# Softmax weights of two more pairs turned on TensorE, conversions taken off GpSimd, norm read from PSUM

## The chip, the cores and the metric

One core of one Trainium2 chip. The metric is the device time of one execution in microseconds (us).

## The reference, cut to what matters

```python
scores = scale * q @ k^T; scores = where(mask, -1e9, scores)      # 2 batches, 12 heads, 448 x 448, causal
attn = exp(scores - max) / (sum + 1e-9); x = attn @ v              # x: 896 tokens x 768
xn = x / sqrt(mean(x * x) + 1e-6) * rms_g
x = (silu(xn @ w_gate) * (xn @ w_val)) @ w_out                     # 768 -> 1536 -> 768
return ((x @ w1) * (x @ w2)) @ w3 @ w_out2                         # 768 -> 1024 -> 1024 -> 768
```

All data are fp32.

## The kernel before, in words

Every fp32 matrix outside the scores is split into a high part (fp16, "hi") and the rest (bf16, "lo"), and every product is three 16-bit matmuls: hi*hi, hi*lo, lo*hi. The kernel has two parts.

*Part one, 0 to about 168 us.* Attention runs over 12 pairs of heads (`pair`: 6 for each batch). For a pair, TensorE (PE) makes four blocks of scores in fp32, VectorE (DVE) adds the mask and takes the minimum (L556), ScalarE (ACT) takes the exponential (L560). The softmax weights then have to be turned (transposed) before they meet V. There are two ways. `turn` (L591): four 128x128 fp32 transposes on PE into a bank (L596), then ACT takes hi (L599) and DVE takes lo from the bank (L601); four such turns make one pair. `send` (L605): hi (L442/443/444) and lo (L447/448) are taken first in SBUF, and a DMA on SyncE's queue (SP) turns both 16-bit halves (L608); three such transfers make one pair, two of 128 x 1536 and one of 128 x 1024 elements. `DA` and `DB` name the pairs that are sent. Then PE multiplies with V (720 small matmuls, "PV"), and DVE divides by the row sum (L657 to L661).

In the same part the product of the last two weight matrices is formed (`w_prime`: 384 matmuls of 384 columns, evicted by ACT at L516) and the first gate weights are read. Each weight piece comes by DMA into one of four `st` buffers (L459), and two DVE instructions and one ACT instruction rebuild an fp32 number from its 64-bit form (`fetch`, L461, L464, L468).

At the end of each batch `norm` scales by the root mean square: ACT sums squares (L669), DVE and GpSimd (POOL) make the reciprocal root, DVE spreads it into `diag` (L684), PE multiplies each 128 columns with it (six groups into three banks), ACT evicts the bank with the gain (L700), and hi and lo are taken from the evicted fp32. For the second batch `mix` (L711) forms the seven operand sums of a Strassen-Winograd product out of both batches.

*Part two, from 168.67 us to the end.* 1944 matmuls of 448 columns: 12 units of gate and value, the down projection, 8 units of w1 and w2, 3 units of the last product. Each unit's weights are fetched, summed (L482) and split; its seven products are joined by DVE (L818).

The order of all instructions comes from a planner (`Plan`): it walks the graph with a price for each operation on each engine that may do it, places every operation on an engine and in a row, and repeats this eight times with priorities from the walk before. `alt` lists the engines that may also do an operation; for hi parts these are DVE and POOL, for lo parts and sums POOL. Buffers of SBUF that DVE and POOL share are priced as a lock (`port`). PE gets idle fillers (L432) in the first 60 us where the walk sees a gap. The numbers at the head (`TP`, `PO`, `BIAS`, `THETA` and so on) set the first priorities and the willingness to move work.

Of the kernel before, what the change touches and what calls it, by code (L numbers as in the profile page):

```python
# [15 lines left out]
ALU = mybir.AluOpType  # L16
# [23 lines left out]

TP = 28.0521
WP0 = -244.6493
WPS = 48.9793
GVS = 6.4864
OS = 3.1806
AS = 4.3573
FS = -5.7914
PO = dict(dq=86.1608, dv=18.1427, vh=-4.1615, vl=31.153, sc=-23.1187, s3=-45.5392, hA=-61.1976, hl=15.902,
    hB=-24.2123, pv=19.2543, sq=-20.7221, nm=29.1952, wm=26.8125, ww=-36.4818, wx=25.6973, g=24.6307,
    a=-40.6597, o=14.4327, f=-41.7402, gm=-30.163, e=10.5623, ae=-45.2952, y=-25.9701, t1=23.8236,  # L50
    mx=19.799, dw=-6.0874)


PASSES = 8
BIAS = {"dve": 17.4016, "pool": 80.0945, "act": 139.3857}
THETA = 0.4843

DA, DB = range(3,12), range(3,12)

# [6 lines left out]
class Plan:  # L66
# [39 lines left out]
    def schedule(self, ways, deps, prio, forward):  # L106
# [71 lines left out]
        while done < n:  # L178
            t, e = min((max(free[e], first[e]), e) for e in free if ready[e] and e not in idle)
            i = next((i for _, i in ready[e] if avail[i][e] <= t and not declines(t, e, i)), None)  # L180
            if i is None:
                idle.add(e)
                continue
            if e == "dve" and ways[i][e][2] and port > t:
                i = next((q for _, q in ready[e] if avail[q][e] <= t and not ways[q][e][2]), i)
            idle.clear()
            done += 1
            pop(i)
            us, _, locks = ways[i][e]
            if e == "pe":  # L190
                while forward and t - free[e] > 0.5 and t < FILL and cols.get(int(free[e] / TICK), 0.0) < 1.15 * WARM:
                    warm.append(free[e])
                    free[e] += pe(free[e], 0.215, 1.0)
                t = max(t, free[e])
                us = pe(t, us, self.ops[i][3])
            if locks:
                t = max(t, port)
                port = t + us
            if e == "dve":
                locked = locks  # L200
            free[e] = t + us
            start[i], pick[i] = t, e
            for u in users[i]:
# [66 lines left out]
def dma_us(b):  # L270
    return b / 310.0e3


@with_exitstack
def fused_kernel(ctx: ExitStack, tc, qk, v, g, wgv, wo, wab, w3t, wout, out):
# [253 lines left out]
    def pair(b, gi):  # L529
# [144 lines left out]
    def norm(b):  # L674
# [11 lines left out]
            rstd[b].to_broadcast([P, NT, P]), op=ALU.mult), r=[("rstd", b), "ident"], w=["diag"], prio=pr, port=True)  # L686
        ys = {}
        for gi in (0, 3, 1, 4, 2, 5):
# [3 lines left out]
            def f(x4=x4, ps=ps):  # L692
# [261 lines left out]
```

## Time and profile before

| | us |
|---|---|
| time before, median of 3 | 550.02 (549.77 to 550.32) |
| the profiled execution's own time | 548.47 |
| its span, first to last instruction | 546.7 |
| busy: PE, DVE, ACT, POOL | 524.3, 495.8, 338.8, 237.5 |
| TensorE's granted clock, mean | 1.000 |

The profiled execution is 1.77 us longer than its span and 1.55 us shorter than the median of the runs. Busy PE includes matmuls in flight, so 96% busy is not 96% of PE's peak. The granted clock is at full speed, 2.4 GHz, in every slice but the very end.

### The profile page before, as it was taken

The numbers are of one execution on the slowest core, as the hardware profiler recorded it, in microseconds if no ns is written. First come the engines' busy times: TensorE is split into PE (matmuls) and PEld (weight loads), VectorE is DVE, ScalarE is ACT, GpSimd is POOL, SyncE is SP. The second block draws the span as 40 slices with busy tenths as digits, with TensorE's granted clock in tenths as the row PEclk, the third lists the DMA queues.
The fourth block names the chain that finished last, engine by engine and source line by source line (L and its number), as shares of the span: only waits on it lengthen the run. The fifth ranks groups of instructions, "written<-read, shape, count | busy, mean of one in ns | idle before, by whom it ended". The sixth has DMA issues, their size and how long they took to land.

```text
span 546.7 us, 9215 instructions
## 1 busy us (share of the span) xinstructions
PE 524.3 (96%) x3442; PEld 286.6 (52%) x3442; DVE 495.8 (91%) x909; ACT 338.8 (62%) x492; POOL 237.5 (43%) x198
## 2 busy tenths in 40 slices
PE   6899999999899999999999999999999999999997
PEld 4565565564666554444555455555555555454553
DVE  6999999989959999999999999899658999999953
ACT  5988887896678676557464767676336553633210
POOL 4534364676453837053656420140211846673400
PEclk9999999999999999999999999999999999999999
DMA  8888799999951133334242446517104211000021
GB/s 276 288 278 263 222 252 218 258 248 184 279 112 59 34 127 130 122 109 173 70 162 78 158 172 252 208 59 236 52 0 168 65 59 59 0 1 0 35 101 68
DMA packets 55197, 77.02 MB, mean 141 GB/s; under 512 B 39792, under 2 KB 41328, under 8 KB 55152
## 3 DMA queue, kind: packets, MB, share of 16 engines
q1 hardware_dynamic: 55152, 76.43, 48.1%
q8 instruction: 27, 0.44, 0.3%
q14 instruction: 18, 0.15, 0.1%
HBM read 64.23 MB, written 2.75 MB: 123 GB/s over the span
## 4 chain that ended last, share of the span: by engine, by line
PE 54%; DVE 23%; DMA 8%; issue 5%; ACT 3%; POOL 0%; DVEq 0%; SPq 0%; ACTq 0%
PE bank L486 54%; DVE arena L818 6%; DVE arena L447 6%; DMA arena<-arena 5%; DVE cv L468 3%; DVE st L482 3%; DVE cv L461 2%; DVE arena L482 2%; DMA st<-in_wout 2%; ACT st L464 1%; DMA st<-in_w3t 1%; DVE arena L556 1%; ACT arena L442 1%; ACT arena L560 1%; DVE arena L547 0%
## 5 line engine op out<-in xcount | busy, mean ns | idle before, releaser
L486 PE MATMUL bank<-arena 128*128 128x448 f16 (+10 forms) x2976 | 446.1, 315 | 14.7 <-ACT wpr L516 3.9
L486 PEld LDWEIGHTS <-arena 128*128 128x128 f16 x3048 | 248.8, 98 | 229.0 <-issue 22.1
L464 ACT ACTIVATE st<-st 128x768 uint16<-128x768 uint16 (+2 forms) x72 | 117.6, 1658 | 32.6 <-DVE cv L461 29.9
L818 DVE TENSOR_TENSOR arena<-bank,arena 128x448 f32<-128x448 f32 x161 | 92.1, 612 | 18.1 <-PE bank L486 17.8
L442 ACT ACTIVATE arena<-arena 128x448 f16<-128x448 f32 (+2 forms) x90 | 53.9, 612 | 40.4 <-DVE arena L482 27.8
L468 DVE SCALAR_TENSOR_TENSOR cv<-st,cv 128x768 int32<-128x768 int32 (+2 forms) x84 | 75.1, 903 | 2.8 <-ACT st L464 2.6
L448 POOL TENSOR_TENSOR arena<-arena 128x448 bf16<-128x448 f32 (+2 forms) x29 | 49.6, 1713 | 56.7 <-ACT arena L442 44.5
L486 PE MATMUL bank<-xs,arena 128*128 128x448 f16 x360 | 72.4, 353 | 1.7 <-ACT arena L815 1.1
L447 DVE TENSOR_TENSOR arena<-arena 128x448 bf16<-128x448 f32 (+2 forms) x80 | 61.2, 780 | 2.4 <-ACT arena L442 1.1
L442 ACT ACTIVATE arena<-cv 128x768 f16<-128x768 f32 (+2 forms) x61 | 41.0, 679 | 32.5 <-DVE cv L468 18.6
L461 DVE TENSOR_SCALAR cv<-st 128x768 int32<-128x768 int32 (+2 forms) x84 | 50.0, 600 | 7.3 <-DMA st<-in_wout 4.2
L448 POOL TENSOR_TENSOR arena<-cv,arena 128x384 bf16<-128x384 f32 (+2 forms) x31 | 44.4, 1434 | 24.8 <-ACT arena L442 24.2
L483 POOL TENSOR_TENSOR arena<-arena 128x448 f32<-128x448 f32 x23 | 30.1, 1314 | 35.6 <-DVE arena L818 21.3
L560 ACT ACTIVATE arena<-arena 128x384 f32<-128x384 f32 (+3 forms) x84 | 41.2, 518 | 5.8 <-DVE arena L556 5.2
L444 POOL TENSOR_SCALAR arena<-cv 128x384 f16<-128x384 f32 (+2 forms) x22 | 20.2, 918 | 55.7 <-DVE cv L468 31.1
L447 DVE TENSOR_TENSOR arena<-cv,arena 128x768 bf16<-128x768 f32 (+2 forms) x53 | 43.3, 824 | 0.8 <-POOL arena L444 0.7
L447 DVE TENSOR_TENSOR arena<-st,arena 128x1536 bf16<-128x1536 f32 (+1 forms) x25 | 42.1, 1682 | 0.1
L482 DVE TENSOR_TENSOR arena<-arena 128x448 f32<-128x448 f32 x57 | 37.5, 668 | 4.1 <-ACT arena L864 4.1
L442 ACT ACTIVATE arena<-st 128x1536 f16<-128x1536 f32 (+1 forms) x22 | 30.5, 1389 | 17.4 <-DVE st L482 7.7
L556 DVE CUSTOM_DVE_ANT_0 arena<-bank,arena 128x384 f32<-128x384 f32 (+3 forms) x84 | 35.7, 441 | 1.9 <-PE bank L486 1.2
L486 PEld LDWEIGHTS bank<-arena 64*128 64x128 f32 (+2 forms) x288 | 27.5, 178 | 19.0 <-issue 5.2
L815 ACT ACTIVATE arena<-bank 128x448 f32<-128x448 f32 x23 | 12.6, 546 | 25.3 <-PE bank L486 15.2
(69 smaller groups left out, 310.2 us busy)
## 6 DMA issues: line engine op xcount, KB each, us to landing
st<-in_wgv SPq DMA_DIRECT2D x24, 768.0 KB, 4.5
st<-in_wab SPq DMA_DIRECT2D x16, 768.0 KB, 4.4
st<-in_wo SPq DMA_DIRECT2D x12, 768.0 KB, 4.4
st<-in_w3t SPq DMA_DIRECT2D x16, 512.0 KB, 4.8
st<-in_wout SPq DMA_DIRECT2D x16, 384.0 KB, 3.9
arena<-in_qk SPq DMA_DIRECT2D x12, 448.0 KB, 5.1
arena<-in_v SPq DMA_DIRECT2D x12, 256.0 KB, 3.8
out_t<-arena SPq DMA_DIRECT2D x12, 224.0 KB, 1.9
```

The lines of the kernel that those rows point to most:

```text
L442: add("act", act_us(n), lambda: nc.scalar.activation(hi, src, AF.Copy), r=r, w=w, prio=prio, alt=(("dve", dve2_us(n), lambda: nc.vector.te ...
L447: add("dve", dve_us(n), lambda: nc.vector.tensor_tensor(lo, src, hi, op=ALU.subtract), r=r, w=w, prio=prio, port=True, alt=(("pool", pool_ ...
L448: port=True, alt=(("pool", pool_us(n), lambda: nc.gpsimd.tensor_tensor(lo, src, hi, op=ALU.subtract)),))
L461: add("dve", dve2_us(n), lambda: nc.vector.tensor_scalar(cv, hi, 3, 0x3FFFFFFF, op0=ALU.logical_shift_left, op1=ALU.bitwise_and), r=[ks], ...
L464: add("act", ACT_TOP * n - 0.08, lambda: nc.scalar.activation(b[:, :, 2], b[:, :, 1], AF.Copy, scale=1.0 / 8192, bias=-8191.0 / 16384), w= ...
L468: add("dve", dve_us(n), lambda: nc.vector.scalar_tensor_tensor(cv, hi, -0x3FFFFFF9, cv, op0=ALU.bitwise_and, op1=ALU.bitwise_or), r=[ks], ...
L482: add("dve", dve_us(n), lambda: nc.vector.tensor_tensor(out, a, b, op=op), port=True, alt=(("pool", pool_us(n) + 0.1, lambda: nc.gpsimd.te ...
L483: ("pool", pool_us(n) + 0.1, lambda: nc.gpsimd.tensor_tensor(out, a, b, op=op)),), **kw)
L486: nc.tensor.matmul(*a, **k)
L556: add("dve", dve_us(w), lambda: nc.vector.tensor_tensor_reduce(out=sc[:, :w], in0=ss[:, :w], in1=m, scale=-CSC, scalar=3.0e38, op0=ALU.add ...
L560: add("act", act_us(w) + 0.1, lambda: nc.scalar.activation(dst, sc[:, :w], AF.Exp, bias=mx[:, c:c + 1], scale=-1.0), r=[ksc, kmx + (c,)], ...
L818: add("dve", dve_us(S), lambda: nc.vector.tensor_tensor(dst, ps, y, op=ALU.add), r=[kp, ky], w=[kd], prio=p)
```

## The change

- `DA`, `DB`: pairs 5 to 11 are sent by DMA instead of 3 to 11. Pairs 3 and 4 are turned on PE: 6 transfers fewer (27 to 21), 32 transposes of 128x128 more (48 to 80).
- POOL is no longer among the engines of `hi_part` and of V's conversion.
- `norm` no longer evicts the bank to fp32 and splits that: ACT takes hi straight from the bank (`halves`), DVE takes lo, and the differences of `mix`, straight from the bank (`less`, a scalar_tensor_tensor of 448 columns).
- The planner's prices: a transfer that turns 768 columns costs 1.9 us in place of 1.8, one of 512 columns 1.8 in place of 1.4; a plain transfer bytes/390e3 + 0.1 us in place of bytes/310e3, landing 2.4 us later in place of 2.0; POOL waits for the lock before it is given work, and a locked instruction costs 0.02 us more; fillers go where PE would idle over 0.3 us in the first 50 us.
- All numbers at the head are fitted anew, so the order on every engine changes.

```diff
-DA, DB = range(3,12), range(3,12)
+DA, DB = range(5,12), range(5,12)
...
-            t, e = min((max(free[e], first[e]), e) for e in free if ready[e] and e not in idle)
+            t, e = min((max(free[e], first[e], port if e == "pool" else 0.0), e)
+                       for e in free if ready[e] and e not in idle)
...
             if locks:
+                us += TURN
                 t = max(t, port)
...
-LAT = {"pe": 0.25, "sp": 2.0, "dve": 0.12, "act": 0.12, "pool": 0.12}
+LAT = {"pe": 0.25, "sp": 2.4, "dve": 0.12, "act": 0.12, "pool": 0.12}
...
-    return b / 310.0e3
+    return b / 390.0e3 + 0.1
...
     def hi_part(n, hi, src, r, w, prio):
         add("act", act_us(n), lambda: nc.scalar.activation(hi, src, AF.Copy), r=r, w=w, prio=prio, alt=(
-            ("dve", dve2_us(n), lambda: nc.vector.tensor_copy(hi, src)),
-            ("pool", n * 0.00115 + 0.05, lambda: nc.gpsimd.tensor_scalar(hi, src, 1.0, 1.0, op0=ALU.mult, op1=ALU.mult))))
+            ("dve", dve2_us(n), lambda: nc.vector.tensor_copy(hi, src)),))
...
-                 [ktA + (c, j) for c in range(3)], 1.8, t0 + PO["hA"])
+                 [ktA + (c, j) for c in range(3)], 1.9, t0 + PO["hA"])
...
+            def less(dst, kd, y, ky, ps=ps, kp=kp, gc=gc):
+                add("dve", dve_us(S), lambda: nc.vector.scalar_tensor_tensor(
+                    dst, ps[:, :S], gc, y, op0=ALU.mult, op1=ALU.subtract), r=[kp, ky, "gcol"], w=[kd], prio=pr)
+
+            def halves(s, i, ps=ps, kp=kp, gc=gc, less=less):
+                (hi, kh), (lo, kl) = xs(s, i, 0), xs(s, i, 1)
+                add("act", actp_us(S), lambda: nc.scalar.activation(hi, ps[:, :S], AF.Copy, scale=gc),
+                    r=[kp, "gcol"], w=[kh], prio=pr)
+                less(lo, kl, hi, kh)
...
-            if b == 0:
-                part(y, ky, xs, gi // 3, gi % 3, pr)
-            elif gi >= 3:
-                mix(xs, gi % 3, (y0[gi % 3], ("y0", gi % 3)), ys[gi % 3], (y0[gi], ("y0", gi)), ys[gi], pr)
+            if b:
+                t1s[gi] = ew_r.next()
+                less(*t1s[gi], y0[gi], ("y0", gi))
+            else:
+                halves(gi // 3, gi % 3)
```

What the new numbers do to the order is seen at three places. The first is SP's queue where the sent pairs begin: `in_wout` are the last weights of `w_prime`, `in_wgv` the first of the gate units, `in_qk` and `in_v` a pair's inputs. Before:

```order
L459 DMA st3_74<-in_wout 128x768
L540 DMA arena_69<-in_v 128x512
L459 DMA st1_72<-in_wout 128x768
L459 DMA st2_73<-in_wout 128x768
L538 DMA arena_69<-in_qk 128x896
L608 DMA_TRANSPOSE arena_69<-arena_69 128x12x128
L608 DMA_TRANSPOSE arena_69<-arena_69 128x8x128
L608 DMA_TRANSPOSE arena_69<-arena_69 128x12x128
L459 DMA st3_74<-in_wout 128x768
L538 DMA arena_69<-in_qk 128x896
L540 DMA arena_69<-in_v 128x512
L608 DMA_TRANSPOSE arena_69<-arena_69 128x12x128
```

In the change, from the same weights on:

```order
L543 DMA arena_69<-in_qk 128x896
L545 DMA arena_69<-in_v 128x512
L464 DMA st3_74<-in_wout 128x768
L543 DMA arena_69<-in_qk 128x896
L464 DMA st0_71<-in_wgv 128x1536
L543 DMA arena_69<-in_qk 128x896
L464 DMA st1_72<-in_wgv 128x1536
L545 DMA arena_69<-in_v 128x512
L464 DMA st2_73<-in_wgv 128x1536
L543 DMA arena_69<-in_qk 128x896
L612 DMA_TRANSPOSE arena_69<-arena_69 128x12x128 x2
L612 DMA_TRANSPOSE arena_69<-arena_69 128x8x128
```

Three turning transfers of pair 3 and three of pair 4 are gone from among the last `in_wout` pieces; the first transfer that turns now stands behind all weights of `w_prime` and behind three gate weights.

The second place is ACT at the norm of the second batch, from the sums of squares on (128x512 and 128x128 on `arena`, before at L669, now at L673; `wpr` is an eviction of `w_prime`; `bank_65`, `bank_66`, `bank_68` hold the norm's groups). Before:

```order
L669 ACTIVATE arena_69<-arena_69 128x512 x4
L669 ACTIVATE arena_69<-arena_69 128x128
L516 ACTIVATE wpr_70<-bank3_64 128x3x128
L669 ACTIVATE arena_69<-arena_69 128x128 x3
L442 ACTIVATE arena_69<-st0_71 128x1536
L700 ACTIVATE arena_69<-bank4_65,gcol_80 128x448
L700 ACTIVATE arena_69<-bank5_66,gcol_80 128x448
L516 ACTIVATE wpr_70<-bank3_64 128x3x128
L442 ACTIVATE arena_69<-arena_69 128x448
L700 ACTIVATE arena_69<-bank7_68,gcol_80 128x448
L700 ACTIVATE arena_69<-bank4_65,gcol_80 128x448
L700 ACTIVATE arena_69<-bank5_66,gcol_80 128x448
```

In the change:

```order
L673 ACTIVATE arena_69<-arena_69 128x128 x4
L521 ACTIVATE wpr_70<-bank3_64 128x3x128
L448 ACTIVATE arena_69<-cv1_76 128x384
L448 ACTIVATE arena_69<-st0_71 128x1536
L448 ACTIVATE arena_69<-arena_69 128x448
L736 ACTIVATE arena_69<-bank4_65,gcol_80 128x448
L521 ACTIVATE wpr_70<-bank3_64 128x3x128
L710 ACTIVATE arena_69<-bank5_66,gcol_80 128x448
L736 ACTIVATE arena_69<-bank7_68,gcol_80 128x448
L469 ACTIVATE st1_72<-st1_72 128x768
L448 ACTIVATE arena_69<-arena_69 128x448 x2
L710 ACTIVATE arena_69<-bank4_65,gcol_80 128x448
```

Before, every bank is evicted to fp32 (L700) and hi is taken from that (L442); now hi comes from the bank (L710), or is taken from a difference that DVE read from the bank, and an fp32 copy is kept only for three of the six groups (L736). The last-but-one `wpr` eviction moved from between the sums of squares to behind them.

The third place is PE at the same norm: bank 64 holds the last group of `w_prime`, banks 65, 66, 68 the norm, bank 67 the first product of part two. Before, to its end:

```order
L486 MATMUL bank3_64<-arena_69 128x384
L486 MATMUL bank4_65<-arena_69 128x128 x3
L486 MATMUL bank4_65<-arena_69 128x64
L486 MATMUL bank5_66<-arena_69 128x128 x3
L486 MATMUL bank5_66<-arena_69 128x64
L486 MATMUL bank7_68<-arena_69 128x128 x3
L486 MATMUL bank7_68<-arena_69 128x64
L486 MATMUL bank4_65<-arena_69 128x128 x3
L486 MATMUL bank4_65<-arena_69 128x64
L486 MATMUL bank5_66<-arena_69 128x128 x3
L486 MATMUL bank5_66<-arena_69 128x64
L486 MATMUL bank7_68<-arena_69 128x128 x3
L486 MATMUL bank7_68<-arena_69 128x64
L486 LDWEIGHTS arena_69
L486 MATMUL bank6_67<-xs0_81,arena_69 128x448
```

In the change:

```order
L491 MATMUL bank3_64<-arena_69 128x384
L491 MATMUL bank4_65<-arena_69 128x128 x3
L491 MATMUL bank4_65<-arena_69 128x64
L491 MATMUL bank5_66<-arena_69 128x128 x3
L491 MATMUL bank5_66<-arena_69 128x64
L491 MATMUL bank7_68<-arena_69 128x128 x3
L491 MATMUL bank7_68<-arena_69 128x64
L491 LDWEIGHTS arena_69
L491 MATMUL bank6_67<-xs0_81,arena_69 128x448
```

Three of the six groups stand ahead of the first product now; the other three follow between products, and 18 matmuls of part two are done before the last group. Ahead of these rows, 48 matmuls of `w_prime` stand between the last PV and the norm, before it was 39.

Counted over the whole order up to the second `diag`: POOL has 50 instructions in place of 94, DVE 407 in place of 393; up to the last sum of squares ACT has 248 in place of 215 (an accumulating instruction counted once). Fillers go from 58 to 100 matmuls.

## Rows read from the trace of the kernel before

**Rows 1.** The page, part 1: busy time and share of each engine.

```profile
PE 524.3 (96%) x3442; PEld 286.6 (52%) x3442; DVE 495.8 (91%) x909; ACT 338.8 (62%) x492; POOL 237.5 (43%) x198
```

**Rows 2.** Windows of four stretches: us, busy us of each engine (instructions), clock, DMA, GB/s.

```profile
core 0: us, PE busy (x) PEld busy (x) DVE busy (x) ACT busy (x) POOL busy (x), PEclk, DMA share, GB/s
0.00:20.00 20.00, 14.18 (x98) 9.28 (x98) 14.99 (x42) 13.79 (x21) 8.90 (x24) 1.00 0.83 278
0.00:163.00 163.00, 148.81 (x1448) 91.42 (x1449) 143.88 (x393) 131.36 (x237) 85.26 (x94) 1.00 0.95 241
168.67:310.50 141.83, 138.00 (x725) 70.27 (x725) 140.40 (x201) 90.85 (x113) 74.02 (x52) 1.00 0.32 109
461.90:543.00 81.10, 80.39 (x423) 41.06 (x421) 68.27 (x108) 25.61 (x34) 31.52 (x22) 1.00 0.08 31
```

**Rows 3.** Windows up to the last attention matmul and from there to the gate matmuls.

```profile
0.00:156.40 156.40, 142.78 (x1412) 87.90 (x1413) 141.81 (x385) 126.52 (x223) 80.49 (x90) 1.00 0.98 248
156.40:168.67 12.27, 11.69 (x90) 9.08 (x86) 7.30 (x15) 8.70 (x23) 5.48 (x6) 1.00 0.18 54
```

**Rows 4.** Timeline of TensorE: start, length, rows merged by line, idle before.

```profile
153.53 5.35 PE L486 MATMUL bank<-arena 128*128 128x65 f16 x66 [0.57 <-DMA arena<-arena]
159.47 9.37 PE L486 MATMUL bank<-arena 128*128 128x384 f16 x72 [0.58 <-ACT wpr L516]
168.67 2.62 PE L486 MATMUL bank<-xs,arena 128*128 128x448 f16 x13
```

**Rows 5.** ACT by line and form, 0 to 163 us: busy us, mean ns, idle before.

```profile
L442 ACT ACTIVATE arena<-cv 128x512 f16<-128x512 f32 x8 | 5.0, 629 | 3.8 <-DVE cv L468 3.7
L442 ACT ACTIVATE arena<-cv 128x384 f16<-128x384 f32 x9 | 4.6, 519 | 1.6 <-DVE cv L468 1.6
L599 ACT ACTIVATE arena<-bank 128x512 f16<-128x512 f32 x12 | 6.8, 588 | 0.4 <-PE bank L596 0.4
L543 ACT ACTIVATE arena<-arena 128x512 f16<-128x512 f32 x7 | 4.4, 625 | 1.6 <-DMA arena<-in_v 1.6
```

**Rows 6.** DVE by line and form, 0 to 163 us: busy us, mean ns, idle before.

```profile
L447 DVE TENSOR_TENSOR arena<-arena 128x768 bf16<-128x768 f32 x16 | 17.4, 1090 | 1.5 <-POOL st L483 0.8 <-ACT arena L442 0.7
L547 DVE SCALAR_TENSOR_TENSOR arena<-arena 128x512 f16<-128x512 f32 x12 | 10.6, 882 | 0.9 <-ACT arena L543 0.9
L601 DVE TENSOR_TENSOR arena<-bank,arena 128x512 bf16<-128x512 f32 x12 | 8.1, 678 | 0.1
```

**Rows 7.** DVE by source line, 0 to 163 us: shortest, median, longest ns.

```profile
L447 DVE TENSOR_TENSOR arena<-arena x20: 678/952/2130, 68.1 to 146.1; 128x768 bf16<-128x768 f32 x16, 128x512 bf16<-128x512 f32 x4
L547 DVE SCALAR_TENSOR_TENSOR arena<-arena x12: 654/692/1525, 15.3 to 147.8; 128x512 f16<-128x512 f32 x12
```

**Rows 8.** GpSimd (POOL) by line and form, 0 to 163 us.

```profile
L444 POOL TENSOR_SCALAR arena<-arena 128x768 f16<-128x768 f32 x7 | 7.0, 1004 | 10.1 <-ACT arena L560 8.0 <-DMA arena<-arena 2.1
L444 POOL TENSOR_SCALAR arena<-cv 128x512 f16<-128x512 f32 x8 | 6.8, 847 | 18.8 <-DVE cv L468 18.8
L444 POOL TENSOR_SCALAR arena<-cv 128x384 f16<-128x384 f32 x8 | 5.0, 623 | 9.4 <-DVE cv L468 9.4
```

**Rows 9.** TensorE by line and form, 0 to 163 us.

```profile
L432 PE MATMUL bank<-arena 128*128 128x252 f16 x58 | 8.4, 303 | 1.1 <-DVE arena L438 1.1
L596 PE MATMUL bank<-arena 128*128 128x128 f32 x48 | 7.7, 283 | 1.2 <-DVE arena L601 1.1
```

**Rows 10.** The turning transfers by source line: time on the SP queue, shortest, median, longest ns.

```profile
L608 SPq DMA_TRANSPOSE arena<-arena x27: 1231/1527/4877, 69.0 to 148.0; - x27
```

**Rows 11.** DMA issues: KB each, median us from issue to landing.

```profile
st<-in_wout SPq DMA_DIRECT2D x16, 384.0 KB, 3.9
arena<-arena SPq DMA_TRANSPOSE x27, 5.4
```

**Rows 12.** The chain that ended last, by time, 60 to 165 us: start, length.

```profile
79.78 4.90 DMA arena<-arena
94.98 4.27 DMA arena<-arena
```

More of the change, by code (lines that the diff above doesn't have):

```diff
@@ L37 @@
 CSC = 1.0 / 8.0
[L41 to L51, printed above, removed]
+TP = 27.6196
+WP0 = -239.098
+WPS = 45.6507
+GVS = 3.3215
+OS = 5.5733
+AS = 2.8104
+FS = -2.3605
+PO = dict(dq=75.1441, dv=-34.3235, vh=-105.6002, vl=46.2211, sc=-50.0374, s3=-49.1818, hA=-126.5569,
+    hl=33.2591, hB=-20.1561, pv=4.1734, sq=-72.0513, nm=15.7476, wm=1.3462, ww=-44.1947, wx=4.9061,
+    g=68.9761, a=-39.7332, o=0.6949, f=-24.4064, gm=-31.525, e=-8.003, ae=-133.6189, y=-21.9007,
+    t1=-54.0072, mx=44.5005, dw=-92.7682)
 PASSES = 8
-BIAS = {"dve": 17.4016, "pool": 80.0945, "act": 139.3857}
-THETA = 0.4843
-DA, DB = range(3,12), range(3,12)
+BIAS = {"dve": -1.5515, "pool": 164.3712, "act": 123.8607}
+THETA = 0.2478
+DA, DB = range(5,12), range(5,12)
 SQ = ({4: (0, 5, 0), 5: (5, 1, 1)}, {0: (0, 1, 0), 4: (1, 4, 1), 5: (5, 1, 2)})
@@ L190, in schedule @@
             if e == "pe":
-                while forward and t - free[e] > 0.5 and t < FILL and cols.get(int(free[e] / TICK), 0.0) < 1.15 * WARM:
+                while forward and t - free[e] > GAP and t < FILL and cols.get(int(free[e] / TICK), 0.0) < FULL * WARM:
                     warm.append(free[e])
@@ L231, in order @@
         return [f for _, f in sorted(issue, key=lambda x: x[0])]
-LAT = {"pe": 0.25, "sp": 2.0, "dve": 0.12, "act": 0.12, "pool": 0.12}
+LAT = {"pe": 0.25, "sp": 2.4, "dve": 0.12, "act": 0.12, "pool": 0.12}
 SELF = {"pe": 0.0, "sp": 2.0, "dve": 0.127, "act": 0.03, "pool": 0.03}
+TURN = 0.02
 TICK = 3.413
 WARM = 3060.0
-FILL = 60.0
+FILL = 50.0
+GAP = 0.3
+FULL = 2.0
 def mm_us(n):
@@ L544, in pair @@
             r=[kvs], w=[kvh], prio=t0 + PO["vh"], alt=(
-            ("dve", dve2_us(512), lambda: nc.vector.tensor_scalar(vh[:, :, 0:D], vs, SV, 1.0, op0=ALU.mult, op1=ALU.mult)),
-            ("pool", 0.6, lambda: nc.gpsimd.tensor_scalar(vh[:, :, 0:D], vs, SV, 1.0, op0=ALU.mult, op1=ALU.mult))))
+            ("dve", dve2_us(512), lambda: nc.vector.tensor_scalar(vh[:, :, 0:D], vs, SV, 1.0, op0=ALU.mult, op1=ALU.mult)),))
         add("dve", dve_us(512), lambda: nc.vector.scalar_tensor_tensor(
@@ L622, in pair @@
             send(512, *hB_r.next(), pB, [kpB], tB.rearrange("p h c n -> p (h c) n")[:, :, 0:P],
-                 [ktB + (h,) for h in range(2)], 1.4, t0 + PO["hB"])
+                 [ktB + (h,) for h in range(2)], 1.8, t0 + PO["hB"])
         else:
@@ L686, in norm @@
             rstd[b].to_broadcast([P, NT, P]), op=ALU.mult), r=[("rstd", b), "ident"], w=["diag"], prio=pr, port=True)
-        ys = {}
+        ys, t1s = {}, {}
         for gi in (0, 3, 1, 4, 2, 5):
@@ L697, in norm @@
             add("pe", 4 * S / 2400.0 + 0.03, f, r=["diag"] + [kx4 + (j,) for j in range(GH)], w=[kp], prio=pr)
+            gc = gcol[:, gi:gi + 1]
+            def less(dst, kd, y, ky, ps=ps, kp=kp, gc=gc):
[6 more added lines that the diff above has]
+                less(lo, kl, hi, kh)
+            if b and gi >= 3:
+                i = gi % 3
+                t1, k1 = t1s[i]
+                (y, ky), (y2, k2) = ys[i], (y0[gi], ("y0", gi))
+                t2, kt2 = ew_r.next()
+                halves(2, i)
+                less(y, ky, y, ky)
+                less(t2, kt2, t1, k1)
+                tt(y2, y2, t2, ALU.subtract, r=[kt2], w=[k2], prio=pr)
+                part(t1, k1, xs, 3, i, pr + PO["mx"])
+                part(y, ky, xs, 5, i, pr + PO["mx"])
+                part(t2, kt2, xs, 4, i, pr + PO["mx"])
+                part(y2, k2, xs, 6, i, pr + PO["mx"])
+                continue
             y, ky = (y0[gi], ("y0", gi)) if b == 0 else kp_r.next()
             ys[gi] = (y, ky)
-            add("act", actp_us(S), lambda y=y, ps=ps, gi=gi: nc.scalar.activation(
-                y, ps[:, :S], AF.Copy, scale=gcol[:, gi:gi + 1]), r=[kp, "gcol"], w=[ky], prio=pr)
-            if b == 0:
-                part(y, ky, xs, gi // 3, gi % 3, pr)
-            elif gi >= 3:
-                mix(xs, gi % 3, (y0[gi % 3], ("y0", gi % 3)), ys[gi % 3], (y0[gi], ("y0", gi)), ys[gi], pr)
+            if b:
[3 more added lines that the diff above has]
+                halves(gi // 3, gi % 3)
+            add("act", actp_us(S), lambda y=y, ps=ps, gc=gc: nc.scalar.activation(
+                y, ps[:, :S], AF.Copy, scale=gc), r=[kp, "gcol"], w=[ky], prio=pr)
     def part(y, ky, dst, s, i, pr):
```

## The prediction

> **What bounds the kernel now.** I read the windows first, then the timeline of TensorE, then each engine's forms, and the chain last. PE is busy 96% of the span [rows 1], but that counts matmuls in flight, so I cut the span where the kinds of work change. From 168.67 us on there is only one kind, the 448-column matmul [rows 4]. In the first of the two stretches shown PE idles 141.83 - 138.00 = 3.8 us, in the other 81.10 - 80.39 = 0.7 us [rows 2]; nothing in this change alters the 1944 matmuls, so part two can give back some 4.5 us at the very most. Its first stretch is also where DVE is busy 140.40 of 141.83 us: those gaps of PE are DVE's.
>
> What is left is part one, 168.67 us. Up to the last PV at 156.4 us DVE is busy 141.8 us, PE 142.8, ACT 126.5, POOL 80.5, and the DMA engines 0.98 of the time [rows 3]. No engine alone is the bound: they hand each other small pieces in a fixed row, and the fullest, DVE and PE, idle 14.6 and 13.6 us, 5.0 and 5.8 us of it in the ramp of the first 20 us [rows 2]. Then 12.3 us follow from the last PV to the first matmul of part two (168.67 - 156.4), in which PE is busy 11.7 us with the last of `w_prime` and the norm [rows 3, 4]. So the time is about: the moment of the last PV, plus 12.3, plus part two. The granted clock is at full speed in all these stretches [rows 2], so more fillers have no clock to win.
>
> **The change, step by step.** Counts are those of the two orders, up to the second `diag` (ACT: the last sum of squares); durations are from rows. Instructions of one engine overlap by about 0.08 us on DVE and 0.1 us on ACT, an estimate of mine that I take off each mean.
>
> *Conversions off POOL, on ACT.* 28 hi parts and 5 conversions of V leave POOL in part one. With 7.0, 6.8 and 5.0 us for the three big forms [rows 8], and the rest of my count at 0.5 to 0.8 us each, this is some 26 us of POOL; 11 lo parts and sums go as well, about 13 us, so POOL drops from 85 us [rows 2] to some 46. ACT gets 16 more hi parts in part one: 8 of 512 columns and 7 of 384 among them, 8 x 0.53 + 7 x 0.42 = 7.2 us, the others net 1.8, so 9; and 4 conversions of V, 4 x 0.525 = 2.1 us [rows 5].
>
> *Two pairs turned on PE.* 32 transposes at 7.7 / 48 = 0.16 us are 5.1 us of PE [rows 9]. ACT takes hi from the bank, 8 x 0.49 = 3.9 us [rows 5]; DVE takes lo, 8 x 0.60 = 4.8 us [rows 6]. Out go lo parts of 768 columns: on DVE five fewer, 5 x 1.01 = 5.1 us [rows 6]. Six transfers go, each with 1.5 us of SP's queue [rows 10] and 5.4 us to landing [rows 11].
>
> *Norm from the bank.* In part one (first batch) ACT does 12 reads of a bank in place of 6 (the fewer hi parts from SBUF are in the count above), about +3 us at the 0.49 to 0.53 us of the rows nearest to it [rows 5]; DVE gets 6 `less`. No row has this instruction; the nearest is L601, which also reads a bank and an SBUF tensor: 0.678 us for 512 columns [rows 6], so 0.53 for 448 columns after the overlap, 3.2 us. Bounds: nothing, if they stand in idle time, and 6 x 0.88 = 5.3 us by the slowest such form, L547 [rows 6]. For the second batch the chain from bank to operand loses one ACT eviction. What replaces it on PE is neutral by my reading: 9 more matmuls of `w_prime` stand behind the last PV, 18 of part two stand among the norm's groups, and all of them are work that must be done anyway. Bounds 0.5 us faster, 1.5 us slower; I take 0.
>
> *DVE against POOL.* L447 at 768 columns has a mean of 1.090 us against a median of 0.952, L547 0.882 against 0.692, with longest ones of 2.13 and 1.53 [rows 6, 7]: DVE waits for something that is not in its own row, when POOL runs. These 28 instructions lose 16 x 0.14 + 12 x 0.19 = 4.5 us, 16% of their 28.0 us. If only they lose time, it is 4.5 us; if all of DVE's 143.9 us did [rows 2], 23. I take the middle, 14, and of that POOL's cut, 39 / 85: 6.4 us back, bounds 2 and 11. The Trainium skill, page "SBUF — State Buffer", section "SBUF: two separate sides", says that DVE and GpSimd share a port pair under an exclusive lock and that the loser blocks for the whole instruction. By that alone, up to all 39 us taken off POOL could come back to DVE. The trace bears out the direction, not the size: with POOL busy 85 us, the rows put the loss at 4.5 to 23.
>
> DVE's sum for part one: +4.8 - 5.1 + 3.2, other small shifts +2 by my count, so +5 of own work, -6.4 of waiting: about -1.5. ACT's sum: 9 + 2.1 + 3.9 + 3, less 2 for `fetch` and evictions that moved: +16. Then ACT is busy 126.5 + 16 = 142.5 us before the last PV, if that stays at 156.4: 91%, exactly as full as DVE is now (141.8) [rows 3]. DVE comes down to about 140. PE has 5.1 us more of transposes. The 42 more filler matmuls (0.145 us each, 6 us [rows 9]) stand in the first 50 us, where PE idles 5.8 us in the first 20 alone [rows 2]; I cost them at nothing, and if that cover is gone, at up to 4 us.
>
> So three engines can be where one or two are now. **I take the last PV as unmoved: 0 us.** The lower bound: two pieces of the chain, 4.90 and 4.27 us, are turning transfers in the 80 to 100 us stretch [rows 12], where now two pairs fewer wait for one. If their 9.2 us become a turn on PE and its evictions, some 2 us, the last PV comes 7 us sooner. The upper bound: ACT keeps all its 29.9 us of idle time (156.4 - 126.5) and its 16 us come on top.
>
> *Part two.* By my count DVE has some 7 us less and POOL 12 us less to do there, with ACT, at 90.85 of 141.83 us [rows 2], having room for 17 us more. Of PE's 4.5 us of gaps I take 2 us back; bounds 4.5 us back, and 3 us lost to a new order that hands PE its operands late.
>
> **Sum.** 0 + 0 - 2 = -2 us, against the profiled execution's own 548.47 us: 546.5. That execution lies 1.55 us below the median, so the median comes to 550.02 - 2 = **548.0 us**.
>
> **The rivals.**
> *ACT becomes the bound (slower).* ACT is fuller than ever, in a fixed row, and exp, hi parts, evictions of `w_prime` and of turns all queue on it; each exp that waits there holds a score bank, and PE's next scores behind it. If ACT keeps half of the idle time that it cannot keep (16 us too much, so 8 us), the last PV comes 8 us later: 550 + 8 - 2 = 556. It decides once the last PV slips by 3.1 us (2 us from part two and 1.1 us, 0.2% of the time, which is what a measurement of this kernel can tell from no change). For it: DVE, now as full as ACT will be, is followed by PE all through part one. Against: ACT idles for DVE mostly in small pieces.
> *PE pays for the turns and gets nothing (slower).* If the DMA's turns are hidden anyway, 5.1 us of transposes come on top: 550 + 5 - 2 = 553. The Trainium skill, "Advanced Engine Details and Errata", section "X-Bar Transpose (TRN2)", says that transposing DMAs are as fast as regular ones; by that, taking six away buys nothing and this is the outcome. Against it stand the rows: a turn needs 5.4 us to land where a plain 384 KB piece needs 3.9 [rows 11], and it holds SP's queue for 1.5 us [rows 10].
> *Nothing moves.* What DVE gains ACT takes, and part two's gaps stay: 550.
> *The transfers leave the chain (faster still).* The lower bound of the last PV and 2 us of part two: 550 - 7 - 2 = 541. For it: the order puts all of `w_prime`'s weights ahead of the first turn, so transfers that turn no longer share the DMA engines with that stream. Against: the last seven pairs keep their transfers, and PE's wait for the last one, 0.57 us at 153.53 [rows 4], with them.
>
> **How the numbers follow.** Forecast (546 to 549) 0.38; transfers leave the chain 0.17; nothing moves 0.19; ACT becomes the bound 0.19; PE pays 0.07. Faster 0.38 + 0.17 = 0.55, same 0.19, slower 0.26. The range 541 to 556 takes in the middle of every case. The forecast's own range is 546 to 549.
>
> **What would show it.** Right: the last PV within 2 us of 156.4; ACT busy over 140 us before it and DVE at most 141; L447 and L547 means nearer to their medians; POOL under 50 us in part one; PE's idle time after 168.67 us about 2.5 us. Wrong: PE's idle time in part one ended mostly by ACT; gaps of PE among the first products of part two, where the order now waits for three late groups of the norm; or fillers that hold up the first pairs.

## The result, and the profile after

The changed kernel takes 544.12 us (median of 4 runs, 542.50 to 544.86); the kernel before, beside it, 550.14 (549.77 to 550.32). The ratio is 0.9887, 95% interval 0.9865 to 0.9910: 6.0 us faster. The profiled execution took 542.5 us with a span of 540.7; before it was 548.47 and 546.7, so the two profiles differ by 6.0 us too, both at a mean granted clock of 1.000. Two of the six runs of a_dose below took 777.45 and 1399.01 us, in a slow state, and are left out of its ratio; every other run counts.

The page of the changed kernel, part 1 (before: [rows 1]) and the chain that ended last:

```profile
PE 527.1 (97%) x3516; PEld 293.4 (54%) x3516; DVE 487.1 (90%) x923; ACT 363.6 (67%) x540; POOL 179.3 (33%) x137
...
PE 81%; DVE 7%; ACT 5%; DMA 4%; issue 2%; SPq 0%; ACTq 0%; DVEq 0%
```

Windows of the changed kernel, columns as in [rows 2]. The last PV stands at about 153.1 us now: DVE's last division by the row sum (L661 before, L665 after) starts at 154.1 us, before it was at 157.1.

```profile
0.00:20.00 20.00, 16.27 (x110) 11.36 (x111) 13.49 (x36) 14.18 (x23) 5.56 (x19) 1.00 0.87 295
0.00:153.10 153.10, 145.97 (x1480) 93.69 (x1481) 140.09 (x399) 138.58 (x256) 38.73 (x47) 1.00 0.88 241
0.00:163.00 163.00, 154.94 (x1540) 99.70 (x1540) 144.46 (x409) 143.99 (x272) 43.04 (x51) 1.00 0.84 228
172.65:310.00 137.35, 137.35 (x727) 71.05 (x727) 135.71 (x196) 91.35 (x112) 77.14 (x48) 1.00 0.35 115
310.00:460.00 150.00, 150.00 (x795) 77.58 (x794) 134.51 (x205) 95.50 (x111) 25.22 (x16) 1.00 0.35 121
460.00:537.00 77.00, 77.00 (x408) 39.72 (x406) 63.58 (x104) 24.43 (x34) 27.10 (x18) 1.00 0.09 33
```

From 172.65 us on PE is busy without a gap. The timeline of TensorE at the seam (before: [rows 4]):

```profile
151.53 5.00 PE L491 MATMUL bank<-arena 128*128 128x65 f16 x54 [1.08 <-DMA arena<-arena]
157.46 6.68 PE L491 MATMUL bank<-arena 128*128 128x384 f16 x48 [0.93 <-ACT wpr L521]
163.98 1.87 PE L491 MATMUL bank<-xs,arena 128*128 128x448 f16 x9
165.88 1.10 PE L491 MATMUL bank<-arena 128*128 128x128 f32 x8
166.82 1.87 PE L491 MATMUL bank<-xs,arena 128*128 128x448 f16 x9
168.69 2.00 PE L491 MATMUL bank<-arena 128*128 128x128 f32 x16
172.65 2.62 PE L491 MATMUL bank<-xs,arena 128*128 128x448 f16 x13 [1.96 <-DVE arena L705]
```

Products and norm are mixed from 163.98 to 172.65 us, then TensorE waits 1.96 us for DVE's `less` (L705). The trace names no bank; by the rotation of the banks in the kernel (`MB`, `TB`) the next product, the first of the second unit, shares its bank with a group of the norm, which `less` still reads. The rest is one piece in the chain of the changed kernel by time. In that of before the same stretch is split among engines, and its three largest waits of TensorE (second fence) add up to 4.0 us:

```profile
172.65 364.51 PE bank L491 x1926
537.16 0.02 issue
```

```profile
PE bank L486 <- DVE arena L818: 1.6, 3, 0.8
PE bank L486 <- DVE arena L447: 1.3, 2, 0.7
PE bank L486 <- ACT arena L815: 1.1, 1, 1.1
```

This piece gives the price that the prediction lacked: 364.51 / 1926 = 0.1893 us for a matmul of 448 columns, so 1944 need 367.9 us. Before, part two ran from 168.67 to 542.98 us, the end of the last group in PE's timeline: 374.3, **6.4 us more than its matmuls need**. After, it loses nothing behind the norm. 18 of its matmuls (3.4 us) are done before 172.65, so it starts, counted in work, at 172.65 - 3.4 = 169.24: 0.6 us later than before. The sum of the three is the gain: 0.6 us lost at the seam, 6.4 won in part two, 0.2 won in the tail, 6.0 in all.

Not all of the 6.4 us stood as idle time: PE idles 374.33 - 369.80 = 4.5 us there. PE's timeline of the kernel before in the gate units shows why:

```profile
224.59 2.19 PE L486 MATMUL bank<-arena 128*128 128x448 f16 x9
226.61 1.87 PE L486 MATMUL bank<-xs,arena 128*128 128x448 f16 x9
...
242.01 2.24 PE L486 MATMUL bank<-xs,arena 128*128 128x448 f16 x11
244.89 3.20 PE L486 MATMUL bank<-xs,arena 128*128 128x448 f16 x16 [0.63 <-DVE arena L447]
247.93 1.87 PE L486 MATMUL bank<-arena 128*128 128x448 f16 x9
```

Read from start to start, 9 matmuls take 9 x 0.1893 = 1.70 us when they run freely (226.61 to 228.31 does). The 9 at 224.59 took 2.02, 0.32 too much, and no idle time is shown at all. The 11 at 242.01 took 2.88 where 2.08 would do: 0.80 lost, 0.63 of it shown.

DVE and POOL by form, from 163 us to the end: before (L447, L448, L444), then after (L452, L453).

```profile
L447 DVE TENSOR_TENSOR arena<-st,arena 128x1536 bf16<-128x1536 f32 x18 | 33.0, 1836 | 0.1
L448 POOL TENSOR_TENSOR arena<-st,arena 128x1536 bf16<-128x1536 f32 x1 | 3.5, 3512 | 2.4 <-ACT arena L442 2.4
L444 POOL TENSOR_SCALAR arena<-cv 128x768 f16<-128x768 f32 x4 | 7.2, 1807 | 25.1 <-PE bank L486 22.2 <-DVE cv L468 2.9
L444 POOL TENSOR_SCALAR arena<-arena 128x448 f16<-128x448 f32 x3 | 3.7, 1226 | 14.7 <-DVE arena L482 14.5
```

```profile
L452 DVE TENSOR_TENSOR arena<-st,arena 128x1536 bf16<-128x1536 f32 x14 | 25.9, 1852 | 0.1
L453 POOL TENSOR_TENSOR arena<-st,arena 128x1536 bf16<-128x1536 f32 x5 | 15.5, 3106 | 8.2 <-DVE arena L449 4.4 <-ACT arena L448 3.8
```

Four lo parts of 1536 columns went from DVE to POOL, 7.1 us of DVE, in the room of conversions that POOL no longer makes in part two. That is most of what DVE has less to do over the whole kernel, 8.7 us (495.8 to 487.1). It is read from the two traces; that these four lo parts are what gives the gain is not tested by a run.

### The profile page after: what moved, and what is told of

Same layout as the page of the kernel before. It is cut to its first block, busy times and chain, and to the rows that moved or that the text cites. A ratio compares the mean times of both kernels' runs of the same rounds, so it can differ in the third digit from the quotient of the medians.

```text
span 540.7 us, 9343 instructions
## 1 busy us (share of the span) xinstructions
PE 527.1 (97%) x3516; PEld 293.4 (54%) x3516; DVE 487.1 (90%) x923; ACT 363.6 (67%) x540; POOL 179.3 (33%) x137
## 4 chain that ended last, share of the span: by engine, by line
PE 81%; DVE 7%; ACT 5%; DMA 4%; issue 2%; SPq 0%; ACTq 0%; DVEq 0%
PE bank L491 80%; DMA st<-in_wout 2%; DVE arena L452 1%; ACT st L469 1%; PE bank L600 1%; ACT arena L448 1%; DMA arena<-arena 1%; DVE arena L560 1%; DVE cv L473 1%; DMA st<-in_wgv 1%; DVE cv L466 1%; DMA arena<-in_v 1%; ACT arena L736 1%; ACT arena L564 1%; ACT arena L673 0%
## 5 line engine op out<-in xcount | busy, mean ns | idle before, releaser
L448 ACT ACTIVATE arena<-arena 128x448 f16<-128x448 f32 (+2 forms) x96 | 57.0, 612 | 35.9 <-DVE arena L487 27.2
L453 POOL TENSOR_TENSOR arena<-cv,arena 128x384 bf16<-128x384 f32 (+2 forms) x29 | 46.1, 1590 | 86.8 <-ACT arena L448 77.8
L448 ACT ACTIVATE arena<-cv 128x384 f16<-128x384 f32 (+2 forms) x82 | 54.0, 670 | 23.7 <-PE bank L491 11.9
L453 POOL TENSOR_TENSOR arena<-arena 128x448 bf16<-128x448 f32 (+2 forms) x32 | 46.6, 1468 | 49.4 <-ACT arena L448 40.7
L466 DVE TENSOR_SCALAR cv<-st 128x768 int32<-128x768 int32 (+2 forms) x84 | 45.3, 547 | 12.2 <-DMA st<-in_wout 4.4
L452 DVE TENSOR_TENSOR arena<-arena 128x448 bf16<-128x448 f32 (+2 forms) x68 | 50.5, 753 | 1.8 <-ACT arena L448 1.4
L448 ACT ACTIVATE arena<-st 128x1536 f16<-128x1536 f32 (+1 forms) x25 | 34.4, 1381 | 19.5 <-DVE st L487 9.9
L452 DVE TENSOR_TENSOR arena<-cv,arena 128x384 bf16<-128x384 f32 (+2 forms) x55 | 44.2, 815 | 0.2 <-ACT arena L448 0.2
L564 ACT ACTIVATE arena<-arena 128x128 f32<-128x128 f32 (+3 forms) x84 | 41.6, 520 | 2.8 <-DVE arena L560 2.2
L488 POOL TENSOR_TENSOR st<-cv,st 128x384 f32<-128x384 f32 x8 | 10.8, 1353 | 78.3 <-DVE st L487 78.3
L560 DVE CUSTOM_DVE_ANT_0 arena<-bank,arena 128x128 f32<-128x128 f32 (+3 forms) x84 | 35.9, 443 | 0.4 <-ACT arena L564 0.3
L452 DVE TENSOR_TENSOR arena<-st,arena 128x1536 bf16<-128x1536 f32 (+1 forms) x21 | 35.3, 1679 | 0.1
L488 POOL TENSOR_TENSOR arena<-arena 128x448 f32<-128x448 f32 x18 | 24.9, 1388 | 14.6 <-ACT arena L871 5.8
L871 ACT ACTIVATE arena<-arena 128x448 f32<-128x448 f32 x24 | 13.7, 575 | 19.1 <-DVE arena L850 19.0
```

Source lines behind the costliest of these rows:

```text
L452: add("dve", dve_us(n), lambda: nc.vector.tensor_tensor(lo, src, hi, op=ALU.subtract), r=r, w=w, prio=prio, port=True, alt=(("pool", pool_ ...
L453: port=True, alt=(("pool", pool_us(n), lambda: nc.gpsimd.tensor_tensor(lo, src, hi, op=ALU.subtract)),))
L466: add("dve", dve2_us(n), lambda: nc.vector.tensor_scalar(cv, hi, 3, 0x3FFFFFFF, op0=ALU.logical_shift_left, op1=ALU.bitwise_and), r=[ks], ...
L488: ("pool", pool_us(n) + 0.1, lambda: nc.gpsimd.tensor_tensor(out, a, b, op=op)),), **kw)
L560: add("dve", dve_us(w), lambda: nc.vector.tensor_tensor_reduce(out=sc[:, :w], in0=ss[:, :w], in1=m, scale=-CSC, scalar=3.0e38, op0=ALU.add ...
L564: add("act", act_us(w) + 0.1, lambda: nc.scalar.activation(dst, sc[:, :w], AF.Exp, bias=mx[:, c:c + 1], scale=-1.0), r=[ksc, kmx + (c,)], ...
```

## The experiments

The theory after the result (G): the gain is DVE's backlog in part two, which held PE back, and is gone. Rivals: GpSimd's conversions no longer hold up DVE in part one (C); the two pairs turned on TensorE, or the norm from the bank, are what is needed (T). The kernel before was run beside every set: 549.24 us with the first (a_oldnorm to a_oldplan), 549.52 with the second (b_cut, a_dose, b_conv_act, a_bank), 549.45 with the third (the three fitted ones and a_cut).

### DVE's work in part two, less and more

Each of the three kernels keeps the order of the kernel it comes from. In b_cut and a_cut the lo parts of the weights that are 1536 columns wide are left out in favour of a copy, which takes about half as long; in a_dose half of each is done a second time. `other` replaces what an instruction on DVE does; the planner's prices stay. The lines that carry `other` into the order are left out here.

```diff
-        add("dve", dve_us(n), lambda: nc.vector.tensor_tensor(lo, src, hi, op=ALU.subtract), ...
+        i = add("dve", dve_us(n), lambda: nc.vector.tensor_tensor(lo, src, hi, op=ALU.subtract), ...
+        if n == 1536:                                    # b_cut (from before), a_cut (from after)
+            pl.other[i] = lambda: nc.vector.tensor_copy(lo, src)
+        if n == 1536:                                    # a_dose (from after)
+            pl.other[i] = lambda: [nc.vector.tensor_tensor(lo[:, :k], src[:, :k], hi[:, :k], ...) for k in (n, 768)]
```

**b_cut.** 

> The kernel before in its own order, but the lo parts of 1536 columns that VectorE makes (19, ten of them in the gate stage) are plain conversions of half the length: VectorE is 0.8 us lighter for each, 15 us in all; the lo parts are not the reference's. Theory G (VectorE is the bound of the gate stage and its lag is the 6.5 us that TensorE loses after the norm): those 6.5 us fall to 2 or less, 544 to 546 us. Rival (the order of the products causes the gaps, not VectorE's load): 549 us or more.

Measured 543.61 us, ratio 0.9891 [0.9846, 0.9937]: the whole gain of the change, in the order of before.

**a_cut.** 

> The changed kernel in its own order, but each lo part of 1536 columns on DVE (15 of them) is a plain copy of about half its length; lo parts of the weights are then not the reference's. In the kernel before the same cut brought 6.5 us. Theory G, after the change DVE no longer holds TensorE back in part two: within 1.0 us of the changed kernel, 543.1 to 545.1, and no gap of TensorE but the one behind the norm. Rival: some of DVE's lag is left, hidden in stretched matmuls: 541.5 us or less.

Measured 543.81 us, ratio 0.9910 [0.9881, 0.9940]. The same cut is worth 6 us before the change and nothing after it.

**a_dose.** 

> The changed kernel in its own order, but behind each of the 15 lo parts of 1536 columns on VectorE half of it is done again: 13 us more of VectorE, 6 of them in the gate stage. Theory G with little margin: TensorE's gaps come back, 3 to 6 us more than the changed kernel's 544.1. Rival (the change left VectorE with more than 6 us of margin there): within 1 us of 544.1.

Measured 554.07 to 556.36 us in four runs, ratio 1.0091 [1.0053, 1.0129], 2% above that of the changed kernel. That is more than either theory expected.

Windows over part two, from its first product to the end of its last, of before, b_cut, after, a_cut and a_dose:

```profile
168.67:543.00 374.33, 369.80 (x1946) 189.64 (x1945) 346.08 (x509) 203.62 (x248) 151.56 (x103) 1.00 0.29 100
```

```profile
169.88:538.00 368.12, 368.08 (x1946) 190.11 (x1945) 332.19 (x508) 204.02 (x248) 141.41 (x103) 1.00 0.29 101
```

```profile
163.98:537.20 373.22, 371.16 (x1970) 192.74 (x1969) 341.08 (x515) 219.21 (x268) 135.58 (x86) 1.00 0.29 100
```

```profile
163.25:536.40 373.15, 371.16 (x1970) 192.74 (x1969) 330.00 (x514) 218.97 (x268) 131.52 (x86) 1.00 0.28 100
```

```profile
168.01:551.00 382.99, 374.35 (x1970) 192.89 (x1969) 357.27 (x528) 218.47 (x268) 135.91 (x86) 1.00 0.28 98
```

In the order of before, DVE's 346.1 us cost PE 6.4 us and 332.2 cost it nothing. In the order of after (whose window holds the rest of the norm, 5.3 us) 330.0 and 341.1 give the same length, 373.2, and 357.3 us make it 9.8 us longer. So 16.2 us more of DVE cost PE 9.8. If a us of DVE past the point where PE starts to wait costs PE no more than a us, the change left a margin of 16.2 - 9.8 = 6.4 us at most. (In a_dose part one is 4 us later as well; its granted clock is 0.91 in the first 20 us and 0.97 from 100 to 165, so I read nothing from that.)

Theory G is shown in both orders: less work on DVE in part two gives the gain in the old one, more takes it back in the new one. Two limits stand. b_cut takes 13.9 us off DVE, the change 9.3 (351.9 to 342.7 from 163 us to the end), so whether the smaller cut is enough in the old order is not tested. And in b_cut POOL's same 103 instructions take 10.2 us less as well; the next run speaks against that as the cause.

### GpSimd's conversions on ACT, in the order of before

```diff
+        for i, w in enumerate(ways):                     # b_conv_act
+            if pick[i] == "pool" and next(iter(w)) == "act":
+                pick[i] = "act"
```

**b_conv_act.** 

> The kernel before in its own order, place for place, but ScalarE does the 49 conversions that GpSimd did (44 hi parts, 5 of V). Theory C (GpSimd's conversions hold VectorE up): VectorE's means for two-operand subtractions fall and the time is 2 to 6 us shorter, 544 to 548 us. Rival A (what ScalarE takes on stands in front of exponentials and costs as much): 550 us or more, up to 556, the last attention matmul later by as much.

The trace has 44 such conversions, 39 hi parts and 5 of V. Measured 556.64 us, ratio 1.0131 [1.0081, 1.0181]. The windows up to 163 us (before: [rows 2]), up to 169 us, and over part two, then two of DVE's forms up to 163 us ([rows 6]), and what DVE waits for most:

```profile
0.00:163.00 163.00, 145.34 (x1416) 89.33 (x1417) 140.03 (x389) 141.68 (x257) 53.07 (x57) 0.99 0.94 238
0.00:169.00 169.00, 150.77 (x1448) 92.49 (x1449) 141.66 (x393) 146.46 (x270) 57.74 (x61) 0.99 0.91 233
174.67:550.00 375.33, 369.87 (x1946) 189.67 (x1945) 346.05 (x510) 210.12 (x258) 135.71 (x93) 1.00 0.28 99
```

```profile
L450 DVE TENSOR_TENSOR arena<-arena 128x768 bf16<-128x768 f32 x16 | 16.3, 1019 | 1.0 <-ACT arena L445 1.0
L550 DVE SCALAR_TENSOR_TENSOR arena<-arena 128x512 f16<-128x512 f32 x12 | 9.8, 820 | 0.1
```

```profile
DVE arena L559 <- ACT arena L563: 8.1, 15, 1.9
```

The window up to 163 us holds four instructions of DVE fewer than before, because this kernel is late; its 140.03 us can't be set against 143.88. The same 393 instructions are done by 169 us: 141.66 us. So 27.5 us less of POOL (33 conversions, 85.26 to 57.74) gave DVE 2.2 us back. The relief is real and small. But DVE now waits 8.1 us for exponentials (L563) that stand in ACT's row with the new conversions, and part one comes out 6.0 us longer (first product at 174.67). Theory C falls as a cause by itself: in part one of this order the conversions cost more on ACT than they free on DVE. In part two POOL has 15.9 us less to do (151.56 to 135.71), DVE is as busy as before (346.05 us), and the stretch takes 375.3 us, no less than before. So less work on POOL changes nothing there; less work on DVE does.

### One part undone, ordered anew, not fitted

Each is the changed kernel with one thing as before (a_bank: with two banks exchanged), and the planner makes a new order with the changed kernel's numbers.

```diff
-        (norm of the changed kernel)                     # a_oldnorm
+        (norm of the kernel before)
+            ("pool", n * 0.00115 + 0.05, lambda: nc.gpsimd.tensor_scalar(hi, src, 1.0, 1.0, ...)),   # a_poolconv, V likewise
-DA, DB = range(5,12), range(5,12)                        # a_nine
+DA, DB = range(3,12), range(3,12)
-(prices, rules and numbers of the changed kernel)        # a_oldplan
+(those of the kernel before)
-MB = (3, 6, 7, 0, 1, 2, 4, 5)                            # a_bank
+MB = (3, 6, 7, 5, 1, 2, 4, 0)
```

**a_oldnorm.** 

> The changed kernel with the norm of before (evict each bank to fp32, then split and mix in SBUF); all else, the fitted numbers too, as in the change; the planner lays out a new order. Theory N (the norm read from the bank is what freed VectorE ahead of the gate stage, so that TensorE no longer waits there): the idle time of TensorE after the norm comes back, 4 to 6 us, 548 to 550 us. Rival P (the prices and the fit did it): within 1.5 us of the changed kernel's 544.1, TensorE without gaps in the gate stage.

Measured 557.38 us, ratio 1.0142 [1.0099, 1.0185].

**a_poolconv.** 

> The changed kernel with GpSimd again allowed to do hi parts and V's conversion; numbers and prices of the change. Theory C (conversions on GpSimd cost VectorE its port): if the planner gives GpSimd 20 or more conversions, VectorE's means for subtractions rise and the time with them, 547 to 550 us. Rival P: the planner, which prices the lock, places them where they don't hurt: within 1.5 us of 544.1.

Measured 553.38 us, 1.0068 [1.0045, 1.0092].

**a_nine.** 

> The changed kernel with nine pairs turned by DMA (pairs 3 to 11) in place of seven; numbers and prices of the change. Theory T (the two pairs' transfers stood on the path of part one): the last attention matmul comes 2 to 7 us later than in the change, 546 to 551 us. Rival: TensorE saves 5 us of transposes and the transfers are hidden, 540 to 544 us.

Measured 556.02 us, 1.0131 [1.0076, 1.0185].

**a_oldplan.** 

> The changed kernel's operations (seven pairs, no conversions on GpSimd, norm from the bank) with the prices, rules and fitted numbers of before. Theory P (the prices and the fit carry the gain): 548 to 552 us, TensorE idle again in the gate stage. Rival (the three changes of operations carry it): 543 to 546 us.

Measured 565.48 us, 1.0293 [1.0246, 1.0341].

**a_bank.** 

> The changed kernel with two PSUM banks exchanged in the rotation of the products (3, 6, 7, 5, 1, 2, 4, 0), so that the product which waited 1.96 us behind the norm need not wait for a bank that VectorE still reads. The planner lays a new order with numbers that were not fitted for it. If the new order is as good as the old one: 541 to 543 us. If an order whose numbers were not fitted is worse for that alone, as the four runs before suggest: 547 to 557 us.

Measured 551.52 us, 1.0028 [1.0005, 1.0050].

All are slower than the kernel before, by 0.3 to 2.9%, though none differs from the changed kernel in more than one of its parts. The first four lie above the times of both theories in their expectations. a_bank, which only changes the order in which products take banks, loses 1.4% against the changed kernel. TensorE does 36 matmuls of part two there ahead of its wait for L705 instead of 18, but then waits 2.1 us all the same. In a_poolconv GpSimd takes 37 conversions, and DVE's mean for a subtraction of 768 columns up to 163 us rises only from 997 to 1036 ns. So these runs measure mostly that numbers fitted to one set of operations make a bad order for another. a_oldplan says one thing more: the new operations alone, under the prices and numbers of before, cost 2.9%.

### The same three, fitted anew

The numbers at the head (`TP`, `PO`, `BIAS` and so on) were searched again for each: change a few at random, keep them if the planner's walk ends no later.

**a_nine_fit.** 

> The changed kernel with nine pairs sent again instead of seven, and the numbers at the head fitted anew for it. Theory T, two pairs turned on TensorE are needed: the turning transfers of pairs 3 and 4 come back into the chain and the last PV into the region of 156 us, 546.5 us or more. Rival F, the fit is what counts and any of these sets of operations can be ordered about as well: within 2 us of 544.1, that is 542.1 to 546.1. As it stood without a fit, 556.02.

Measured 553.44 us, ratio 1.0049 [1.0015, 1.0083].

**a_oldnorm_fit.** 

> The changed kernel with the norm of the kernel before (bank evicted to fp32, halves taken from that), and the numbers at the head fitted anew for it. Theory T, the norm from the bank is needed: DVE and ACT pay for 6 evictions and 6 subtractions of 448 columns more and the first product starts later, 547 us or more. Rival F: 542.1 to 546.1. Without a fit it was 557.38.

Measured 554.27 us, 1.0078 [1.0049, 1.0107].

**a_poolconv_fit.** 

> The changed kernel with GpSimd allowed to convert hi parts and V, and the numbers at the head fitted anew for it. Theory T, no conversions on GpSimd are needed, since they hold up DVE: 547 us or more. Rival F: 542.1 to 546.1. Without a fit it was 553.38.

Measured 558.35 us, 1.0164 [1.0119, 1.0208].

By the bounds set ahead theory T holds in all three. I don't read it so: with the fit a_poolconv became 5 us slower on the chip than without, so a better walk is not a better order, and the fit scatters as much as the effect I looked for. All three lose in part two; a_nine_fit and a_oldnorm_fit also come to their first product later than the changed kernel, by 5.3 and 7.1 us (169.30 and 171.09 in place of 163.98). TensorE's waits in part two of a_nine_fit (the others have DVE at the head of the list too):

```profile
PE bank L488 <- DVE arena L847: 6.2, 5, 1.9
PE bank L488 <- DVE arena L449: 0.9, 2, 0.6
PE bank L488 <- ACT arena L733: 0.5, 1, 0.5
```

Part two is 11.9, 10.5 and 20.8 us longer than its matmuls (a_nine_fit, a_oldnorm_fit, a_poolconv_fit), what is left of the norm among it; after the change it is 5.3. What each of the three parts is worth under an order as good as that of the changed kernel stays open.

## Why the prediction was right, and where not

The time, 548.0 with a range of 541 to 556, holds 544.12, which lies between the forecast and the rival "the transfers leave the chain"; the forecast's own range, 546 to 549, does not. The gain's place was right, its size was not.

**Part two, -2 us: right in mechanism, mis-sized.** It gave 6.4. The prediction said that it "can give back some 4.5 us at the very most", by PE's idle time [rows 2]. That bound was wrong: busy time holds stretched matmuls, so idle time is a lower bound of what an engine loses. The right reading was at hand: a free group of 9 from start to start in PE's timeline, times 216 groups. The prediction also put all of those gaps down to DVE; 1.1 us of the 4.0 listed above ended with ACT (L815). The step under it, DVE's work there some 7 us less, was close: 8.7 us less over the whole kernel, and none of it before 163 us (143.88 before, 144.46 after).

**Last PV unmoved, 0: it came 3.0 us sooner,** by the last division (157.1 to 154.1), inside the bounds of -7 to +16, but outside the 2 us that the prediction named as a sign of being right.

**Norm, 0, bounds -0.5 to +1.5: it took the 3.0 us back, and 0.6 more.** 9 more matmuls of `w_prime` behind the last PV are some 9 x 6.68 / 48 = 1.3 us of work that was moved from ahead of it (an estimate; the row holds matmuls of the norm too); the wait of 1.96 us for L705 is new, and is the "gaps of PE among the first products of part two" that the prediction named as a way to be wrong. Two terms taken as zero missed by 3 us each in opposite directions. 1.3 us of that is the same work on the other side of the mark; that the rest cancels was luck.

**ACT as full as DVE was: right.** 138.58 of 153.1 us is 90.5%, where DVE had 141.8 of 156.4; it stays under the 140 us named as a sign, because the last PV came sooner. It didn't become the bound in this order: of PE's waits up to the first product 1.9 us end with ACT, before 3.9. In b_conv_act, with 141.7 us up to 163 in an order not made for it, DVE waits for ACT and part one grows by 6.0 us. So that rival was a fair one.

**Relief of DVE from POOL, 6.4 us, bounds 2 to 11: 2.2 by b_conv_act** for a cut of 27.5 us of POOL, at the lower bound. The prediction took 39 us of POOL off; at the same rate that is 3.1. The Trainium skill, "SBUF — State Buffer", section "SBUF: two separate sides", makes the loser of the port block for a whole instruction; by that up to 27.5 us could have come back (an estimate). The run agrees with the direction and puts the size at 0.08 us for each us of POOL. POOL fell to 43.0 us in part one, as predicted (under 50). The means were half right: two of DVE's forms after the change, and one line's shortest, median and longest ([rows 6, 7]):

```profile
L452 DVE TENSOR_TENSOR arena<-arena 128x768 bf16<-128x768 f32 x11 | 11.0, 997 | 1.0 <-ACT arena L448 0.7 <-ACT arena L564 0.3
L551 DVE SCALAR_TENSOR_TENSOR arena<-arena 128x512 f16<-128x512 f32 x12 | 10.4, 870 | 0.0
```

```profile
L551 DVE SCALAR_TENSOR_TENSOR arena<-arena x12: 658/684/1489, 11.1 to 147.4; 128x512 f16<-128x512 f32 x12
```

The first came from 1090 to 997 ns, the second stayed (882 to 870). Its longest runs beside POOL work that is left: DVE's and POOL's timelines at 128 us:

```profile
128.26 1.49 DVE L551 SCALAR_TENSOR_TENSOR arena<-arena 128x512 f16<-128x512 f32 x1
```

```profile
128.20 1.00 POOL L488 TENSOR_TENSOR st<-cv 128x384 f32<-128x384 f32 x1
129.28 1.32 POOL L488 TENSOR_TENSOR st<-st,cv 128x384 f32<-128x384 f32 x1
```

**`less`, 0.53 us:** 0.675 on average over six (L705), 0.6 without the overlap; 3.6 us in place of 3.2.

**The transfers:** their share of the chain fell from 5% to 1%; between 60 and 165 us it had five turning transfers, 28.8 us, and has one, 5.8. But PE's own waits for them up to the first product rose from 0.9 to 1.5 us, and the last PV's wait for one (0.57 us before, [rows 4]) became 1.08. What shrank are PE's waits for a pair's inputs (`in_qk`, 3.3 to 0.6 us) and for evictions of `w_prime` (3.9 to 1.9). Whether the transfers or something else moved the last PV by 3 us no run here separates.

**PE pays:** it didn't. PE is busy 145.97 us up to the last PV, 3.2 more than before, but idles 7.1 us there (153.1 - 145.97) instead of 13.6; after 168.67 us it idles 1.96 us, predicted 2.5.

## What to carry to other kernels

Bound what a stretch can give back by its count of instructions times the time of one in a free run, not by the idle time that is shown. Where one engine follows another closely, a few us of work on the one that leads decide: cut its work in the old order with everything else unchanged before arguing about the new order. Compare the busy time of an engine over the same instructions, not over the same us. And where the order is fitted to its operations, undoing one of them measures the fit, not the operation.

## What was not expected of the hardware

The relief of DVE from GpSimd is small: 0.08 us for each us of GpSimd taken away in part one, and none in part two (b_conv_act). The other way it is larger: in b_cut, with 17 subtractions of DVE in part two replaced by copies, GpSimd's same 103 instructions there took 141.4 us in place of 151.6. And the mean granted clock differs between executions of one kernel: in a_oldnorm's four it was 0.990, 0.993, 0.997 and 0.999, with spans of 557.9, 556.2, 555.0 and 552.8 us, so an interval over several runs tells more there than one profile.
